# A planned lag before transposes and value products, and a dearer change of tiling, in a fused attention and gated MLP kernel

## The chip, the cores and the metric

The kernel runs on one core of a Trainium2 chip. The metric is the time of one execution on the device in microseconds (us); lower is better. Matrix products run on PE (TensorE), elementwise work on DVE (VectorE), ACT (ScalarE) and a little on POOL (GpSimd); SP issues the loads and stores.

## The reference

Inputs are `q`, `k`, `v` of 4 batches x 8 heads x 768 positions x 64, and three weight matrices of the MLP. In short:

```python
scores = scale * q @ k^T + bias           # bias falls with distance, one slope per head
scores = where(is_global | is_local, scores, -1e9)   # 8 global keys, 96 local keys back
a      = softmax(scores)
x      = (a @ v), heads side by side      # 3072 tokens x 512
out    = ((x @ w_a) * (x @ w_b)) @ w_out  # 512 -> 1536 -> 512
```

Attention is sparse: a block of 128 queries needs the first keys and the 96 before it, so 256 key columns (128 for the first block of a batch). Everything is fp32 on the outside; the large products split each operand in a high and a low part (`xh`, `xl`; `hh`, `hl`; the two halves of `wt`) and add three products. The weights arrive as 64-bit words and are turned into fp32 and split on ACT and DVE first.

## The kernel before

The 24 query blocks of 128 tokens are cut into eight units of 4, 2, 3, 3, 3, 3, 3, 3 blocks. Unit 0's attention stands alone at the start. After it, the MLP of unit *u* runs on PE while the attention of unit *u*+1 is threaded between its matmuls. The MLP of a unit loops over 12 slices `f` of the hidden width: two products `p0`, `p1` (L851, 12 matmuls each), a copy of `p0` by ACT into `raw0` (L341), a product with `p1` on DVE (L890), a split into `hh` and `hl`, and the product back into `acc` (L869).

The attention of one head and one block is a chain over four engines: scores on PE (`ps`, L793; L673 in the first two units), subtraction of the distance and a row minimum on DVE (`t`, L537), the exponential on ACT (L553), a sum and a reciprocal on DVE (`sm`, L568 and L575), the normalisation on ACT, DVE or POOL (`t`, L585 or L587), two transposes on PE into `pt` (L609), a copy into `pf` (L341), and, for all blocks of two heads at once, the product with the values on PE (`pa`, L626). Head *h*+2's operands (`qh`, `ql`, `kk`) are split by DVE and ACT meanwhile. The scores use the array as 128 rows x 128 columns, the values as 128 x 64 (two heads side by side in the array), the scores of the first two units as 64 x 128: each is another tiling of the array.

No order is written by hand. Every step is an `Op` with a due time, a price in ns on each engine that can do it, and the buffers it reads and writes. `Schedule.order` plays the program with these prices: an engine that is free takes, of the steps whose inputs are ready, the one with the earliest due time whose buffers fit; a step's result counts as ready for the next after a lag per engine (`LAGS`: PE 200 ns, ACT 270, DVE 230, POOL 290). What comes out is only the order in which each engine's instructions stand, and which engine does a step that several can do. On the chip each engine then follows its list and waits on semaphores where an input is not there. A step that the plan thinks ready too early therefore holds up everything behind it on its engine, and any change of a price or a lag moves the whole plan from there on.

Transposes are planned by `turn`, value products by `values`; `Plan` holds a unit's blocks, and `paired` is true for units 0 and 1.

Of the kernel before, what the change touches and what calls it, by code (L numbers as in the profile page):

```python
# [24 lines left out]
P = 128  # L25
# [17 lines left out]
SPLITLEAD = 3000  # L43
SLACK = 1.5
BACKLOG = 1.0
PRICE = {"dve": 2.0, "pool": 2.0}
TRACE = False
LAGS = {"pe": 200.0, "act": 270.0, "dve": 230.0, "pool": 290.0, "dma": 2300.0}
# [12 lines left out]
class Plan:  # L61
# [3 lines left out]

    def __init__(self, blocks, paired):
        self.nb = len(blocks)
        self.kkeys = []
        self.vkeys = []
        self.kwin = []  # L70
        self.vslot = []
        self.parts = []
        for n, (b, blk) in enumerate(blocks):
            if blk == 0:
                keys = np.arange(P)
            else:
                q0 = blk * P
                keys = np.concatenate([np.arange(G), np.arange(q0 - LW, q0 + P)])
            joined = blk == 1 and n > 0
            if paired and n % 2 == 0:  # L80
                self.parts.append(len(self.kkeys))
            if joined:
                self.kwin.append((self.kwin[-1][0], 2 * P))
                self.kkeys += [(b, j) for j in keys[P:]]
                self.vslot.append([self.vslot[-1][0], len(self.vkeys)])
                self.vkeys.append((b, keys[P:]))
            else:
                self.kwin.append((len(self.kkeys), len(keys)))
                self.kkeys += [(b, j) for j in keys]
                slots = []  # L90
                for c in range(len(keys) // P):
                    slots.append(len(self.vkeys))
                    self.vkeys.append((b, keys[c * P : (c + 1) * P]))
                self.vslot.append(slots)
        self.nk = len(self.kkeys)
        self.nv = len(self.vkeys)
        self.k0 = self.nb * P
        self.ncol = self.k0 + self.nk // 2
        if paired:

            ends = self.parts[1:] + [self.nk]
            self.pieces = []
            at = 0
            for k, end in zip(self.parts, ends):
                self.pieces.append((at, at + 2 * P - k, 2 * P + end - k, (k, end)))
                at += 2 * P + end - k
            self.ncol = at
# [41 lines left out]


class Op:
    def __init__(self, index, due, costs, emit, reads, writes, late, port):
        self.index, self.due, self.costs, self.emit, self.late = index, due, costs, emit, late
        self.port = port
        self.bufs, self.after, self.before = [], [], 0
        self.ready, self.engine = 0.0, None
        found = {}
        for is_write, keys in ((False, reads), (True, writes)):
            for key in keys:
                buf, part = key if isinstance(key, tuple) else (key, None)  # L160
                if buf not in self.bufs:
                    self.bufs.append(buf)
                for other, p, w in buf.log:
                    if (w or is_write) and other is not self and (p == part or p is None or part is None):
                        found[other.index] = other
                buf.log.append((self, part, is_write))
        for other in found.values():
            other.after.append(self)
            self.before += 1
        for buf in self.bufs:  # L170
            buf.left += 1


class Schedule:
# [11 lines left out]
        self.tags.setdefault(b.tag, []).append(b)  # L186
        return b

    def op(self, due, emit, reads=(), writes=(), late=0.0, port=(), **costs):

        self.ops.append(Op(len(self.ops), due, costs, emit, reads, writes, late, port))

    def order(self):
        free = {e: 0.0 for e in self.SYNC}
        ready = {e: [] for e in self.SYNC}
        heap = []
        head = {t: 0 for t in self.tags}
        live = {t: 0 for t in self.tags}
        taken = set()
        out = []  # L200
        now = 0.0
        port = 0.0

        def arrive(op):
            for e in op.costs:
                insort(ready[e], (op.due, op.index, op))

        def fits(op):
            for b in op.bufs:
                if b in taken:  # L210
                    continue
                queue = self.tags[b.tag]
                if head[b.tag] >= len(queue) or queue[head[b.tag]] is not b or live[b.tag] >= b.bufs:
                    return False
            return True

        def wins(op, e):
            if len(op.costs) == 1:
                return True
            at = {}  # L220
            for o, c in op.costs.items():
                at[o] = max(free[o], now) + c * PRICE.get(o, 1.0)
                for due, index, other in ready[o]:
                    if (due, index) >= (op.due, op.index):
                        break
                    if len(other.costs) == 1 and fits(other):
                        at[o] += BACKLOG * other.costs[o]
            return at[e] <= min(at.values()) + 40.0

        for op in self.ops:  # L230
            if not op.before:
                arrive(op)
        while len(out) < len(self.ops):
            started = True
            while started:
                started = False
                for e in free:
                    if free[e] > now:
                        continue
                    for item in ready[e]:  # L240
                        op = item[2]
                        if e in op.port and port > now:
                            continue
                        if fits(op) and wins(op, e):
                            break
                    else:
                        continue
                    for o in op.costs:
                        ready[o].remove(item)
                    for b in op.bufs:  # L250
                        if b not in taken:
                            taken.add(b)
                            head[b.tag] += 1
                            live[b.tag] += 1
                    op.engine = e
                    op.t0 = now
                    out.append(op)
                    free[e] = now + op.costs[e]
                    if e in op.port:
                        port = free[e]  # L260
                    heappush(heap, (free[e], 0, op.index, op))
                    started = True
            if not heap:
                raise RuntimeError("no order")
            now, kind, _, op = heappop(heap)
            if kind == 0:
                for nxt in op.after:
                    if op.engine == "pe" and tuple(nxt.costs) == ("pe",):
                        lag = 0.0
                    else:  # L270
                        lag = self.SYNC[op.engine] + op.late
                    nxt.ready = max(nxt.ready, now + lag)
                    nxt.before -= 1
                    if not nxt.before:
                        heappush(heap, (nxt.ready, 1, nxt.index, nxt))
                heappush(heap, (now + self.SYNC[op.engine], 2, op.index, op))
            elif kind == 1:
                arrive(op)
            else:
                for b in op.bufs:  # L280
                    b.left -= 1
                    if not b.left:
                        live[b.tag] -= 1
        return out, now
# [21 lines left out]
class Fast:  # L306
# [292 lines left out]
                act=act(w) + 100,  # L599
            )  # L600

    def turn(self, due, wins, t, pt, pf):

        nc = self.nc
        w = sum(w for o, w in wins)

        def emit(e):
            for c in range(0, w, P):
                nc.tensor.transpose(pt[:, c : c + P], t[:, c : c + P], self.ident)  # L609

        self.plan.op(due, emit, [t], [pt], pe=w / P * 109)
        self.copy(due, lambda: pf[:, :w], lambda: pt[:, :w], w, [pt], [pf], psum=True)

    def values(self, due, pl, blocks, v, probs, pa):
# [18 lines left out]

        reads = [v] + [probs[s, i][0] for s in range(2) for i in blocks]
        n = sum(len(pl.vslot[i]) for i in blocks)
        self.plan.op(due, emit, reads, [pa], pe=n * 218 + 200)

    def quad(self, u, c, j, due, raw, v, pa, homes):

# [128 lines left out]
    def attention(self, u, start, end):  # L768
        nc, pl, op = self.nc, PLANS[u], self.plan.op
# [7 lines left out]
        for c in range(NCC):  # L777
            probs = {}
            v = self.fetch_v(u, c, start + (2 * c + 1) * step - LOADLEAD)
            for s in range(2):  # L780
# [4 lines left out]
                for i in range(pl.nb):  # L785
# [18 lines left out]
                    self.softmax(h, due, [(0, w)], ps, t, sm)  # L804
                    pt = self.bank("psT", "pt" + n)
                    pf = self.sbuf([P, 2 * P], F32, "pf", "pf" + n, PFBUFS)
                    self.turn(due, [(0, w)], t, pt, pf)
                    probs[s, i] = (pf, 0)
            due = start + (2 * c + 2) * step
            pa = self.bank("psA", f"pa{u}_{c}")  # L810
# [505 lines left out]
```

## Time and profile before

| | us |
|---|---|
| median of 3 runs (lowest, highest) | 778.75 (777.14, 778.99) |
| the profiled execution's own time | 777.36 |
| its span on the core | 775.1 |
| PE busy | 751.5 (97%) |
| DVE busy | 438.7 (57%) |
| ACT busy | 433.7 (56%) |
| unit 0's attention alone, until the first MLP matmul | 38.1 |
| MLP of the last unit, from 695 us on, nothing threaded in | 74.5 |

PE is the engine that the time goes by, and its busy share is near all of the span; but matmul records overlap, so a late matmul is often hidden in a "busy" PE. Two other readings are needed: the time from the start of one matmul to the start of the next, and the idle time of the weight loads (PEld), which stand in PE's queue and wait there for a late input.

### The profile page before, as it was taken

How to read it: one execution, taken by the hardware profiler on the slowest of the kernel's cores; microseconds unless marked ns; L12 is line 12 of the kernel's file. 1: busy time of each engine (PE TensorE's matmuls, PEld its weight loads, DVE VectorE, ACT ScalarE, POOL GpSimd, SP SyncE). 2: the span in 40 equal slices, each digit the busy share in tenths (PEclk: the TensorE clock that was granted, in tenths of full speed). 3: DMA queues.
4: the chain of work that ended last, by engine and by line, in shares of the span. 5: the costliest groups of instructions: out<-in, count | busy, mean ns of one | idle time of the engine just before them, and what ended most of it. 6: DMA issues, size and time to landing. Idle time of an engine off the chain costs nothing.

```text
span 775.1 us, 12558 instructions
## 1 busy us (share of the span) xinstructions
PE 751.5 (97%) x4608; PEld 663.6 (86%) x4608; DVE 438.7 (57%) x1375; ACT 433.7 (56%) x1093; POOL 6.6 (1%) x24
## 2 busy tenths in 40 slices
PE   5799999999999999999999999999999999999997
PEld 4567777798998998989988988999988999889996
DVE  6999999766655654445554554455554545522111
ACT  6999756466656556455555565555544655442111
POOL 1000000000000000000000000000000000000000
PEclk9999999999999999999999999999999999999999
DMA  7888101032221111211112111111112121000001
GB/s 287 334 321 340 35 14 31 32 107 65 75 90 41 62 38 49 72 48 49 43 54 89 42 62 48 48 60 48 52 42 62 62 62 41 0 28 15 1 1 45
DMA packets 20086, 58.04 MB, mean 75 GB/s; under 512 B 2352, under 2 KB 2608, under 8 KB 20016
## 3 DMA queue, kind: packets, MB, share of 16 engines
q1 hardware_dynamic: 20016, 57.16, 21.5%
q8 instruction: 38, 0.62, 0.3%
q14 instruction: 32, 0.26, 0.1%
HBM read 50.86 MB, written 6.29 MB: 74 GB/s over the span
## 4 chain that ended last, share of the span: by engine, by line
PE 84%; DVE 7%; ACT 6%; issue 1%; DMA 1%; ACTq 0%; DVEq 0%
PE p L851 45%; PE acc L869 23%; PE pt L609 5%; PE pa L626 5%; PE ps L793 4%; PE ps L673 1%; ACT wr L418 1%; DVE kk L351 1%; DVE t L537 1%; ACT t L553 1%; ACT t L585 1%; ACT wm L381 1%; DVE wm L408 1%; ACT pf L341 1%; DVE wt L351 1%
## 5 line engine op out<-in xcount | busy, mean ns | idle before, releaser
L851 PE MATMUL p<-xh,wt 128*128 128x384 f32 (+2 forms) x1488 | 438.9, 345 | 4.0 <-DVE wt L343 2.3
L851 PEld LDWEIGHTS p<-xh,wt 128*128 128x128 f32 x1488 | 272.9, 189 | 18.2 <-issue 3.6
L851 PE MATMUL p<-xl,wt 128*128 128x384 f32 (+2 forms) x816 | 269.8, 342 | 0.2 <-DVE xl L351 0.2
L869 PE MATMUL acc<-wt,hh 128*128 128x512 f32 x576 | 206.4, 397 | 0.0
L851 PEld LDWEIGHTS p<-xl,wt 128*128 128x128 f32 x816 | 153.8, 189 | 10.3 <-DVE xl L351 1.4
L890 DVE TENSOR_TENSOR raw<-p,raw 128x384 f32<-128x384 f32 (+2 forms) x96 | 53.4, 557 | 153.5 <-PE p L851 146.8
L869 PEld LDWEIGHTS acc<-wt,hh 128*128 128x128 f32 x576 | 108.3, 188 | 19.0 <-issue 0.5
L553 ACT ACTIVATE t<-t,sm 128x256 f32<-128x256 f32 (+1 forms) x192 | 93.8, 491 | 40.0 <-DVE sm L537 39.0
L869 PE MATMUL acc<-wt,hl 128*128 128x512 f32 x288 | 113.0, 392 | 0.0
L585 ACT ACTIVATE t<-t,sm 128x256 f32<-128x256 f32 (+1 forms) x140 | 68.7, 494 | 71.1 <-DVE sm L575 66.2
L537 DVE CUSTOM_DVE_ANT_0 t<-ps,rel 128x256 f32<-128x256 f32 x160 | 66.6, 421 | 66.9 <-PE ps L793 64.4
L341 ACT COPY raw<-p 128x384 f32<-128x384 f32 (+2 forms) x95 | 45.3, 477 | 70.7 <-PE p L851 70.1
L609 PE MATMUL pt<-ident,t 128*128 128x128 f32 x352 | 68.6, 280 | 5.3 <-ACT t L585 2.5
L341 ACT COPY pf<-pt 128x256 f32<-128x256 f32 (+3 forms) x151 | 56.2, 375 | 22.6 <-PE pt L609 21.6
L351 DVE TENSOR_TENSOR hl<-raw,hh 128x384 fp32r<-128x384 f32 (+2 forms) x96 | 53.4, 556 | 23.7 <-ACT hh L341 23.1
L609 PEld LDWEIGHTS pt<-ident,t 128*128 128x128 f32 x352 | 43.2, 140 | 25.5 <-ACT t L585 10.1
L341 ACT CAST hh<-raw 128x384 fp32r<-128x384 f32 (+2 forms) x85 | 43.6, 513 | 35.9 <-DVE raw L890 34.9
L869 PEld LDWEIGHTS acc<-wt,hl 128*128 128x128 f32 x288 | 54.2, 188 | 6.6
L568 DVE TENSOR_SCALAR sm<-sm 128x1 f32<-128x1 f32 (+1 forms) x168 | 25.7, 153 | 43.5 <-ACT t L553 42.4
L351 DVE TENSOR_TENSOR kk<-raw,kk 64x384 fp32r<-64x384 f32 (+1 forms) x90 | 44.2, 491 | 2.8
L626 PE MATMUL pa<-pf,v 128*64 128x128 f32 x640 | 42.8, 278 | 2.4 <-ACT pf L341 1.9
L626 PEld LDWEIGHTS pa<-pf,v 128*64 128x64 f32 x640 | 34.7, 136 | 11.6 <-issue 5.0
(78 smaller groups left out, 604.7 us busy)
## 6 DMA issues: line engine op xcount, KB each, us to landing
wr<-wts SPq DMA_DIRECT2D x24, 768.0 KB, 12.5
raw<-qkv SPq DMA_DIRECT2D x29, 384.0 KB, 3.0
raw<-qkv SPq DMA_DIRECT2D x24, 320.0 KB, 2.9
v<-qkv SPq DMA_DIRECT2D x16, 384.0 KB, 3.1
out<-o SPq DMA_DIRECT2D x23, 256.0 KB, 2.1
v<-qkv SPq DMA_DIRECT2D x16, 256.0 KB, 2.7
raw<-qkv SPq DMA_DIRECT2D x3, 640.0 KB, 6.0
raw<-qkv SPq DMA_DIRECT2D x1, 256.0 KB, 3.5
```

Of the source, the lines that this page charges most:

```text
L341: self.nc.scalar.copy(out(), src())
L351: lambda e: self.engine(e).tensor_sub(out(), a(), b()),
L537: lambda e, j=j, o=o, w=w, neg=neg: nc.vector.tensor_tensor_reduce(t[:, o : o + w], ps[:, o : o + w], neg[:, :w], -(2.0 ** -(h + 1)), 3.0e ...
L553: lambda e, j=j, o=o, w=w: nc.scalar.activation(t[:, o : o + w], t[:, o : o + w], AF.Exp, bias=sm[:, j : j + 1], scale=-1.0, accum_out=sm[ ...
L568: lambda e: nc.vector.tensor_scalar_add(sm[:, 2 * n : 3 * n], sm[:, n : 2 * n], 1e-9),
L585: nc.scalar.mul(t[:, o : o + w], t[:, o : o + w], r)
L609: nc.tensor.transpose(pt[:, c : c + P], t[:, c : c + P], self.ident)
L626: nc.tensor.matmul(pa[D * s : D * s + D, i * P : i * P + P], v[:, v0 : v0 + D], pf[:, o + c * P : o + c * P + P], start=c == 0, stop=c == ...
L793: nc.tensor.matmul(ps[:, :w], q[:, i * P : i * P + P], kk[:, k0 : k0 + w], start=m == 0, stop=m == 1,)
L851: nc.tensor.matmul(p[:, :T], wt(), b[:, b0 : b0 + T], start=c == 0 and n == 0, stop=c == NCC - 1 and n == 2,)
L869: nc.tensor.matmul(acc[i][:, :], hs[:, i * P : i * P + P], wt(), start=f == 0 and n == 0, stop=f == NF - 1 and n == 2,)
L890: lambda e, asb=asb, pb=pb: nc.vector.tensor_mul(asb[:, :T], pb[:, :T], asb[:, :T]),
```

## The change

Three edits. First, in units 2 to 7 a transpose and a value product count as ready in the plan only 200 ns (`SPARE`) after their inputs' usual lag has passed. The field that carries this replaces `late`, which was always zero; it is now the lag of the step that waits and not of the step that made the input. Secondly, every value product, in all units, is planned 90 ns dearer on PE (290 ns for the change of tiling, not 200). Thirdly, `Plan` keeps whether its unit is one of the later ones. Nothing is computed differently; only orders and the choice of engines can change.

```diff
+SPARE = 200.0
 ...
     def __init__(self, blocks, paired):
         self.nb = len(blocks)
+        self.late = not paired
 ...
                     if op.engine == "pe" and tuple(nxt.costs) == ("pe",):
                         lag = 0.0
                     else:
-                        lag = self.SYNC[op.engine] + op.late
+                        lag = self.SYNC[op.engine] + nxt.spare
                     nxt.ready = max(nxt.ready, now + lag)
 ...
-    def turn(self, due, wins, t, pt, pf):
+    def turn(self, due, wins, t, pt, pf, spare=0.0):
 ...
-        self.plan.op(due, emit, [t], [pt], pe=w / P * 109)
+        self.plan.op(due, emit, [t], [pt], pe=w / P * 109, spare=spare)
 ...
-        self.plan.op(due, emit, reads, [pa], pe=n * 218 + 200)
+        self.plan.op(due, emit, reads, [pa], pe=n * 218 + 290, spare=SPARE if pl.late else 0.0)
 ...
-                    self.turn(due, [(0, w)], t, pt, pf)
+                    self.turn(due, [(0, w)], t, pt, pf, SPARE)
```

The lines of the changed file stand five lines further down than those of the file before (L609 becomes L614, L851 becomes L856).

The order moves in three places that matter below. The first is PE in the MLP of unit 2, around the transposes of unit 3's head 5, block 2 (`pt3_5_2`); `p02_8` and `p12_8` are the two products of hidden slice 8. Before:

```order
L851 MATMUL p02_8_3274<-xh2_2584,wt8_0_1219 128x384
L851 MATMUL p02_8_3274<-xl2_2593,wt8_0_1219 128x384
L851 MATMUL p02_8_3274<-xh2_2584,wt8_0_1219 128x384
L609 MATMUL pt3_5_2_3325<-ident_91,t3_5_2_3279 128x128 x2
L851 MATMUL p12_8_3282<-xh2_2584,wt8_1_1250 128x384
L851 MATMUL p12_8_3282<-xl2_2593,wt8_1_1250 128x384
L851 MATMUL p12_8_3282<-xh2_2584,wt8_1_1250 128x384
```

Now:

```order
L856 MATMUL p02_8_3283<-xh2_2569,wt8_0_1215 128x384
L856 MATMUL p02_8_3283<-xl2_2586,wt8_0_1215 128x384
L856 MATMUL p02_8_3283<-xh2_2569,wt8_0_1215 128x384
L856 MATMUL p12_8_3291<-xh2_2569,wt8_1_1247 128x384
L856 MATMUL p12_8_3291<-xl2_2586,wt8_1_1247 128x384
L856 MATMUL p12_8_3291<-xh2_2569,wt8_1_1247 128x384
L614 MATMUL pt3_5_2_3330<-ident_91,t3_5_2_3278 128x128 x2
```

Three matmuls of the MLP have moved ahead of the two transposes.

The second place is ACT near the end of unit 0's attention, from the first weight tile's preparation on (`wm`, `wr`: steps of preparing weights; `wt0_0`: the first finished weight tile; `t1_0_3_0`: the normalised probabilities of a head in the fourth pair). Before:

```order
L381 ACTIVATE wm0_0_504<-wr0_0_283 128x768
L418 ACTIVATE wr0_0_283<-wr0_0_283 128x768
L341 CAST xh0_337<-pa0_2_463 128x512
L341 COPY pf0_0_3_0_522<-pt0_0_3_0_509 128x384
L341 COPY pf1_0_3_0_526<-pt1_0_3_0_516 128x384
L381 ACTIVATE wm0_1_528<-wr0_1_317 128x768
L418 ACTIVATE wr0_1_317<-wr0_1_317 128x768
```

Now:

```order
L386 ACTIVATE wm0_0_497<-wr0_0_278 128x768
L346 COPY pf0_0_3_0_510<-pt0_0_3_0_493 128x384
L590 ACTIVATE t1_0_3_0_454<-t1_0_3_0_454,sm1_0_3_0_455 128x128
L590 ACTIVATE t1_0_3_0_454<-t1_0_3_0_454,sm1_0_3_0_455 128x256
L346 CAST xh0_334<-pa0_2_475 128x512
L423 ACTIVATE wr0_0_278<-wr0_0_278 128x768
L346 COPY pf1_0_3_0_525<-pt1_0_3_0_519 128x384
L386 ACTIVATE wm0_1_529<-wr0_1_317 128x768
L423 ACTIVATE wr0_1_317<-wr0_1_317 128x768
L346 CAST wt0_0_543<-wm0_0_497 128x768
```

ACT has gained two normalisations and the cast of the first weight tile; DVE did these before.

The third place is ACT a little later, up to the first copy out of the bank `p0` (`raw0<-p00_0`), which frees that bank for slice 1. Before:

```order
L585 ACTIVATE t1_0_3_1_484<-t1_0_3_1_484,sm1_0_3_1_485 128x256
L418 ACTIVATE wr2_0_433<-wr2_0_433 128x768
L418 ACTIVATE wr2_1_458<-wr2_1_458 128x768
L341 COPY pf0_0_3_1_612<-pt0_0_3_1_594 128x512
L341 COPY pf1_0_3_1_618<-pt1_0_3_1_601 128x512
L381 ACTIVATE wm2_0_620<-wr2_0_433 128x768
L418 ACTIVATE wr3_0_487<-wr3_0_487 128x768
L341 CAST xl0_344<-pa0_3_531 128x512
L341 CAST wt1_0_647<-wm1_0_553 128x768
L418 ACTIVATE wr3_1_514<-wr3_1_514 128x768
L418 ACTIVATE wr4_0_544<-wr4_0_544 128x768
L341 COPY raw0_86<-p00_0_561 128x512
```

Now:

```order
L346 COPY pf0_0_3_1_602<-pt0_0_3_1_593 128x512
L423 ACTIVATE wr1_1_393<-wr1_1_393 128x768
L386 ACTIVATE wm2_0_617<-wr2_0_424 128x768
L346 COPY pf1_0_3_1_619<-pt1_0_3_1_611 128x512
L346 CAST wt1_0_624<-wm1_0_561 128x768
L423 ACTIVATE wr2_0_424<-wr2_0_424 128x768
L423 ACTIVATE wr2_1_457<-wr2_1_457 128x768
L346 CAST xl0_344<-pa0_3_534 128x512
L386 ACTIVATE wm2_1_653<-wr2_1_457 128x768
L346 CAST wt1_1_657<-wm1_1_589 128x768
L423 ACTIVATE wr3_0_488<-wr3_0_488 128x768
L346 COPY raw0_86<-p00_0_553 128x512
```

Ahead of the copy there now stand the cast `wt1_1` and the step `wm2_1`, which came after it, while `wr3_1` and `wr4_0` have moved behind it.

More of the change, by code (lines that the diff above doesn't have):

```diff
@@ L151, with __init__ @@
 class Op:
-    def __init__(self, index, due, costs, emit, reads, writes, late, port):
-        self.index, self.due, self.costs, self.emit, self.late = index, due, costs, emit, late
+    def __init__(self, index, due, costs, emit, reads, writes, spare, port):
+        self.index, self.due, self.costs, self.emit, self.spare = index, due, costs, emit, spare
         self.port = port
@@ L187, in buf, with op @@
         return b
-    def op(self, due, emit, reads=(), writes=(), late=0.0, port=(), **costs):
-        self.ops.append(Op(len(self.ops), due, costs, emit, reads, writes, late, port))
+    def op(self, due, emit, reads=(), writes=(), spare=0.0, port=(), **costs):
+        self.ops.append(Op(len(self.ops), due, costs, emit, reads, writes, spare, port))
     def order(self):
```

## The prediction

> **What bounds the kernel now.** I read the page's head first, then the stretches, then who waits for whom on PE and its weight loads, then the instructions in order of time.
>
> ```profile
> span 775.1 us, 12558 instructions
> PE 751.5 (97%) x4608; PEld 663.6 (86%) x4608; DVE 438.7 (57%) x1375; ACT 433.7 (56%) x1093; POOL 6.6 (1%) x24
> PE 84%; DVE 7%; ACT 6%; issue 1%; DMA 1%; ACTq 0%; DVEq 0%
> ```
>
> PE holds 84% of the chain that ended last. Where the other engines hold it shows in the table of stretches (columns: length, busy time and count of PE, PEld, DVE, ACT, POOL, then granted clock, DMA share, GB/s):
>
> ```profile
> 0.00:38.10 38.10, 25.01 (x208) 17.76 (x208) 29.55 (x145) 30.83 (x95) 2.20 (x18) 0.96 0.80 309
> 38.10:50.70 12.60, 10.89 (x57) 7.71 (x57) 12.14 (x24) 12.45 (x20) 0.00 (x0) 0.86 0.75 278
> 50.70:156.00 105.30, 104.70 (x516) 82.43 (x517) 99.90 (x194) 75.14 (x136) 0.00 (x0) 1.00 0.29 112
> 227.00:322.00 95.00, 94.46 (x592) 85.63 (x592) 49.48 (x167) 53.22 (x140) 0.74 (x1) 1.00 0.17 51
> ```
>
> Until 50.7 us PE is not the bound: in the second stretch DVE (12.1 of 12.6 us) and ACT (12.45) are full and PE issues 57 rows. From 50.7 on PE is, with DVE at 95% in the rest of unit 0's MLP and about half busy later. So two kinds of gain or loss count: whatever moves the 50.7, and every late input of PE behind it.
>
> The late inputs of the units from the third on show as waits of weight loads, which stand in PE's queue (engine, what, released by: us, times, longest; from 160 to 770 us):
>
> ```profile
> PEld pt L609 <- ACT t L585: 8.8, 23, 0.8
> PEld pa L626 <- issue: 4.0, 13, 0.4
> PEld p L851 <- DVE xl L351: 1.4, 5, 0.5
> PEld pt L609 <- ACT pf L341: 1.6, 5, 0.3
> ```
>
> Transposes (`pt`) wait for the normalisation; value products (`pa`) wait for no input of theirs. One late transpose, in order of time:
>
> ```profile
> 287.45 0.74 DVE L343 CAST kk<-raw 64x384 fp32r<-64x384 f32 x2
> 287.76 0.34 PE L851 MATMUL p<-xh,wt 128*128 128x384 f32 x1
> 287.94 0.38 PE L609 MATMUL pt<-ident,t 128*128 128x128 f32 x2
> 288.08 0.42 PE L851 MATMUL p<-xh,wt 128*128 128x384 f32 x1
> 290.05 0.17 DVE L575 RECIPROCAL sm<-sm 128x1 f32<-128x1 f32 x1
> 290.32 0.34 PE L851 MATMUL p<-xh,wt 128*128 128x384 f32 x1
> 290.60 0.51 ACT L585 ACTIVATE t<-t,sm 128x256 f32<-128x256 f32 x1 [1.87 <-DVE sm L537]
> 291.16 0.44 PE L609 MATMUL pt<-ident,t 128*128 128x128 f32 x2 [0.50 <-ACT t L585]
> 291.35 0.42 PE L851 MATMUL p<-xh,wt 128*128 128x384 f32 x1
> ```
>
> A matmul of 384 columns is followed by the next start after 0.18 us (287.76 to 287.94). At 290.32 it is followed after 0.84: 0.66 us are lost, because DVE split the next head's keys before it did the reciprocal (290.05) and ACT normalised only then. The pair of transposes itself then takes 0.19 to the next start and not 0.14. "Idle" says 0.50 here and PEld's wait 0.82, so I use starts.
>
> **Part one: the lag before transposes.** How much is there to gain? 23 waits of 8.8 us, each some 0.16 longer than what PE loses (0.82 against 0.66): 8.8 - 23 x 0.16 = 5.1, and 23 x 0.05 for the slower pair: 6.3 us. Counted block by block from the spacing of starts, 26 of the 144 transposes of units 2 to 7 start 0.04 us or more late, in all 5.6 us; with 26 x 0.05 that is 6.9. I take 6.9 as the pool.
>
> The new order tells how much of it goes. I laid each block's transposes beside its scores and summed the PE rows between them at the spacings above (0.174 us for 384 columns, and in proportion). The mean distance grows from 3.58 to 3.73 us, less than the 0.20 asked for, since PE can only move them by whole steps of three matmuls (0.52 us). Of the 26 late ones 12 stand 0.39 to 0.71 us further off, as `pt3_5_2` does by three matmuls; they hold 3.4 of the 5.6 us, and with 12 x 0.05 that is **-4.0**. 14 stand as before, with 2.3 us; in three of them (block 2 of head 2, units 3, 5 and 7) one cast of keys has left DVE's list between the minimum and the reciprocal, 0.37 us each (two in 0.74 above), more than their 0.20 us of lateness: another **-0.7**. 20 blocks that are on time come closer, for instance `pt5_0_0` and `pt7_0_0` from 5.73 to 3.08 us and `pt2_4_0` from 3.10 to 2.65. The shortest distances that start on time now are 2.8, so a handful become late by 0.1 to 0.3: **+0.6**. Sum of part one: -4.1. Its bounds: -1.5, if as many new ones come late as in the moved list are cured (12 x 0.2 against 4.0); -6.9, if all of the pool goes.
>
> What the moved transposes delay is the copy `pf` and the value products, which have nobody waiting on PE (above); the scores of the next block need another bank and do not stand behind them.
>
> **Part two: the lag and the dearer price of value products.** One visit to the other tiling:
>
> ```profile
> 292.42 0.40 PE L869 MATMUL acc<-wt,hh 128*128 128x512 f32 x1
> 292.75 1.53 PE L626 MATMUL pa<-pf,v 128*64 128x128 f32 x24
> 294.21 0.44 PE L609 MATMUL pt<-ident,t 128*128 128x128 f32 x2
> 295.02 0.39 PE L869 MATMUL acc<-wt,hh 128*128 128x512 f32 x1
> 295.25 0.39 PE L869 MATMUL acc<-wt,hl 128*128 128x512 f32 x1
> ```
>
> Entering costs 0.33 - 0.23 = 0.10 us over the usual spacing of 512 columns, the 24 rows and the way out 1.46: 1.56 in all. The plan charged 6 x 0.218 + 0.20 = 1.51, now 1.60; one is as wrong as the other. The number of value products and of changes of tiling on PE is the same in both orders (87), so no visit is saved. Since they never waited, the lag has nothing to take away. I cost this at 0 in units 2 to 7. What hides it: the result `x` is needed only at the next unit's start, some 10 us after the last block. If that cover went, one value product late by the lag would cost 0.2 + 0.09 us in each of six units: +1.7 at most.
>
> **Part three: what the dearer price does to unit 0.** The 290 holds there too, and from the fourth pair of heads on the orders differ. Here ACT sets PE's start:
>
> ```profile
> 24.01 0.41 ACT L585 ACTIVATE t<-t,sm 128x128 f32<-128x128 f32 x1
> 24.31 0.51 ACT L553 ACTIVATE t<-t,sm 128x256 f32<-128x256 f32 x1
> 35.53 0.98 ACT L418 ACTIVATE wr<-wr 128x768 int32<-128x768 uint32 x1
> 36.33 0.56 ACT L553 ACTIVATE t<-t,sm 128x256 f32<-128x256 f32 x1
> 41.50 0.88 ACT L341 CAST wt<-wm 128x768 fp32r<-128x768 f32 x1
> 42.22 0.57 ACT L585 ACTIVATE t<-t,sm 128x256 f32<-128x256 f32 x1
> 42.63 1.79 ACT L418 ACTIVATE wr<-wr 128x768 int32<-128x768 uint32 x2
> 50.08 0.56 ACT L341 COPY raw<-p 128x512 f32<-128x512 f32 x1
> 50.69 0.50 PE L851 MATMUL p<-xh,wt 128*128 128x512 f32 x1 [0.66 <-ACT raw L341]
> ```
>
> By the starts, a weight step costs ACT 0.80 us, a cast of a weight tile 0.72, a normalisation 0.41 (256 columns) or 0.30 (128). Between the first `wm0_0` and the copy `raw0` ACT gains `wt0_0`, `wt1_1`, `wm2_1`, one normalisation of 128 and two of 256, and loses `wr3_1` and `wr4_0`: 0.72 + 0.72 + 0.80 + 0.30 + 0.82 - 1.60 = +1.76. Before `wm0_0` it loses two normalisations of 256 (to DVE): -0.82. If ACT stays as full as it is, the copy, and with it slice 1 on PE, comes 0.94 later: **+1.0**. Bounds: +1.8, if the 0.82 turns into a wait for DVE, which has taken those two; -0.5, if DVE, freed of the cast `wt0_0` and the two halves of `t1_0_3_0`, lets waits vanish that I do not see.
>
> Sum: -4.1 + 0 + 1.0 = -3.1 us. The profiled execution took 777.36 (span 775.1, and 2.3 around it), so 774.3 for it; it lay 1.4 below the median of the runs, and the same step from the median gives **775.7 us**, 0.4% less. About 0.3%, 2.3 us, is what a measurement of this kernel can tell from no change.
>
> **The rivals.** *The gain is given back in place.* Each plan that moves 87 blocks makes new late ones: 20 come closer, and DVE does five more normalisations of 256 columns over the whole kernel. If part one ends at its lower bound, -1.5 + 1.0: **778.2**, no change. For it speaks that more than half of the late ones stand where they stood; against it that the large ones (0.66, 0.47, four of 0.36 to 0.38) moved.
>
> *The weights become the bound.* In unit 0's MLP DVE is busy 99.9 of 105.3 us; four subtractions of keys and a few casts have moved onto it from POOL and ACT, some 2.5 us at 0.3 to 0.55 each (the cast above is 0.37). It decides once a weight tile's lead over its first matmul is used up: from there each us on DVE is one on PE. Price: the head at +1.8, and the stage by what DVE needs above 105.3 with the waits that it has now, 2.5 to 5 more; with part one as forecast 777.36 - 4.1 + 1.8 + 5 = 780.1, from the median **781.5**, slower. Against it: PE stands with no idle to speak of in that stretch (104.7), so the lead exists.
>
> *A wait in the head drops the clock.*
>
> ```profile
> 35.80:39.20 3.40, 0.73 (x3) 1.00 1.03 422
> 39.20:42.60 3.40, 2.73 (x6) 0.56 1.01 415
> ```
>
> (Columns: PE alone, clock, DMA share, GB/s.) After a stretch in which PE had three rows, the clock stands at 0.56 for the next 3.4 us: 1.5 us lost, though now beside ACT's work. If the longer wait for `raw0` does the same again, it falls on the dense matmuls behind it, where nothing hides it: +1.5, **777.2**. The Trainium skill, "TensorE: Matmul & The Clock Gate", Part 1, says that an idle window of some 3.4 us halves the array's clock until a busy one has passed; this trace agrees with 0.56.
>
> **How the numbers follow.** Forecast 0.52, 775.7 (own range 773.6 to 777.2); given back 0.27, 778.2; clock 0.08, 777.2; weights as the bound 0.13, 781.5. The forecast ends faster by over 0.3% (below 776.4) in some 0.43 of its 0.52, the given-back and clock cases in 0.05 together: faster 0.48, slower 0.12 (nearly all of the weights case), same 0.40. The range goes from 772.8 (part one near its upper bound with the head at 0.5) to 779.8, where half of the slower case is left out.
>
> **What would show it.** Right: PEld's waits for the normalisation between 160 and 770 us fall from 8.8 to some 4 us, `pt3_5_2` starts 0.18 after its forerunner, and slice 1 on PE starts near 51.7 and not 50.7. Wrong: a wait sum that stays near 8, or new waits at `pt` behind DVE's own normalisations; slice 1 before 50.7; or PE idle behind `wt` between 51 and 156 us.

## The result, and the profile after

The changed kernel takes 772.97 us in the median of six runs (771.42 to 774.44), the kernel before 778.82 (777.14 to 778.99). The ratio is 0.993 with a 95% interval of 0.9916 to 0.9943: 5.85 us less, about twice the 3.1 forecast. The time lies 0.2 us inside the range (772.8 to 779.8) and below the narrower one that the prediction gave its forecast (773.6 to 777.2). The two profiled executions lie 4.2 us apart (777.36 and 773.14), nearer to the forecast than the medians are; part of what parts them is told below.

The head of the page of the changed kernel, and its row for the transposes:

```profile
span 771.4 us, 12534 instructions
PE 750.4 (97%) x4608; PEld 666.3 (86%) x4608; DVE 441.0 (57%) x1383; ACT 431.2 (56%) x1088; POOL 4.0 (1%) x21
PE 94%; ACT 3%; DVE 2%; DMA 0%; issue 0%; DVEq 0%; ACTq 0%
L614 PE MATMUL pt<-ident,t 128*128 128x128 f32 x352 | 67.1, 277 | 2.9 <-DVE sm L573 2.0
```

The span is 3.7 us shorter with PE's busy share unchanged: the late matmuls were counted as busy, so this share could not show them. The chain that ended last is PE's own to 94% now, from 84%; this share hangs on the path that the chain takes through the start as well, and the kernel with a lag of 800 ns below has 88%.

Who waits in the queue of PE's weight loads between 160 and 770 us (engine, what, released by: us, times, longest):

```profile
PEld pa L631 <- issue: 5.2, 17, 0.4
PEld pt L614 <- ACT t L590: 3.1, 10, 0.5
PEld p L856 <- DVE xl L356: 1.0, 3, 0.5
PEld pt L614 <- ACT pf L346: 0.8, 3, 0.3
```

The transposes' wait for the normalisation fell from 8.8 us in 23 to 3.1 in 10. The block that the prediction took apart, `pt3_5_2`, in PE's order of time:

```profile
289.92 0.34 PE L856 MATMUL p<-xl,wt 128*128 128x384 f32 x1
290.10 0.34 PE L856 MATMUL p<-xh,wt 128*128 128x384 f32 x1
290.27 0.41 PE L614 MATMUL pt<-ident,t 128*128 128x128 f32 x2
290.44 0.42 PE L856 MATMUL p<-xh,wt 128*128 128x384 f32 x1
```

It starts 0.17 us after its forerunner; before, that was 0.84.

The head of the program, ACT and PE, where slice 1 of unit 0's MLP starts:

```profile
51.85 0.59 ACT L346 COPY raw<-p 128x512 f32<-128x512 f32 x1
52.49 0.50 PE L856 MATMUL p<-xh,wt 128*128 128x512 f32 x1 [0.63 <-ACT raw L346]
```

It starts at 52.5 us, 1.8 later than in the first profile, released by the same copy on ACT.

For all further comparisons I use one sum, taken in the same way from each trace: over the 144 blocks of units 2 to 7, how much later than usual the first transpose starts after the row ahead of it (blocks late by 0.04 us or more), plus what the second transpose of a pair then takes over its 0.109 us. Before, 26 blocks are late by 5.63 us and second transposes cost 1.91: 7.54. After, 10 blocks by 1.53, and 0.93: 2.46.

### The profile page after: what moved, and what is told of

Read it like the earlier page. It is cut to its first block, busy times and chain, and to the rows that moved or that the text cites. A ratio compares the mean times of both kernels' runs of the same rounds, so it can differ in the third digit from the quotient of the medians.

```text
span 771.4 us, 12534 instructions
## 1 busy us (share of the span) xinstructions
PE 750.4 (97%) x4608; PEld 666.3 (86%) x4608; DVE 441.0 (57%) x1383; ACT 431.2 (56%) x1088; POOL 4.0 (1%) x21
## 4 chain that ended last, share of the span: by engine, by line
PE 94%; ACT 3%; DVE 2%; DMA 0%; issue 0%; DVEq 0%; ACTq 0%
PE p L856 52%; PE acc L874 25%; PE pa L631 5%; PE pt L614 5%; PE ps L798 4%; PE ps L678 2%; ACT wr L423 1%; DVE t L542 0%; DMA nv<-ns 0%; DVE kk L356 0%; ACT wm L386 0%; ACT pf L346 0%; ACT t L590 0%; ACT t L558 0%; ACT wt L346 0%
## 5 line engine op out<-in xcount | busy, mean ns | idle before, releaser
L856 PE MATMUL p<-xh,wt 128*128 128x384 f32 (+2 forms) x1488 | 439.7, 346 | 2.0 <-ACT wt L346 1.4
L856 PEld LDWEIGHTS p<-xh,wt 128*128 128x128 f32 x1488 | 273.2, 189 | 16.5 <-issue 3.9
L856 PE MATMUL p<-xl,wt 128*128 128x384 f32 (+2 forms) x816 | 270.4, 342 | 1.1 <-ACT xl L346 0.7
L856 PEld LDWEIGHTS p<-xl,wt 128*128 128x128 f32 x816 | 154.3, 189 | 10.9 <-ACT xl L346 1.1
L895 DVE TENSOR_TENSOR raw<-p,raw 128x384 f32<-128x384 f32 (+2 forms) x96 | 53.4, 556 | 120.5 <-PE p L856 115.7
L558 ACT ACTIVATE t<-t,sm 128x256 f32<-128x256 f32 (+1 forms) x192 | 93.7, 490 | 41.5 <-DVE sm L542 40.5
L590 ACT ACTIVATE t<-t,sm 128x256 f32<-128x256 f32 (+1 forms) x135 | 66.0, 492 | 63.3 <-DVE sm L580 60.4
L614 PE MATMUL pt<-ident,t 128*128 128x128 f32 x352 | 67.1, 277 | 2.9 <-DVE sm L573 2.0
L356 DVE TENSOR_TENSOR hl<-raw,hh 128x384 fp32r<-128x384 f32 (+2 forms) x96 | 53.4, 557 | 24.2 <-ACT hh L346 23.4
L614 PEld LDWEIGHTS pt<-ident,t 128*128 128x128 f32 x352 | 44.3, 140 | 19.2 <-issue 5.2
L356 DVE TENSOR_TENSOR kk<-raw,kk 64x384 fp32r<-64x384 f32 (+1 forms) x94 | 45.8, 487 | 2.9
L631 PEld LDWEIGHTS pa<-pf,v 128*64 128x64 f32 x640 | 34.7, 137 | 12.7 <-issue 6.0
## 6 DMA issues: line engine op xcount, KB each, us to landing
wr<-wts SPq DMA_DIRECT2D x24, 768.0 KB, 12.5
```

What stands on the lines that cost most here:

```text
L356: lambda e: self.engine(e).tensor_sub(out(), a(), b()),
L558: lambda e, j=j, o=o, w=w: nc.scalar.activation(t[:, o : o + w], t[:, o : o + w], AF.Exp, bias=sm[:, j : j + 1], scale=-1.0, accum_out=sm[ ...
L590: nc.scalar.mul(t[:, o : o + w], t[:, o : o + w], r)
L631: nc.tensor.matmul(pa[D * s : D * s + D, i * P : i * P + P], v[:, v0 : v0 + D], pf[:, o + c * P : o + c * P + P], start=c == 0, stop=c == ...
L856: nc.tensor.matmul(p[:, :T], wt(), b[:, b0 : b0 + T], start=c == 0 and n == 0, stop=c == NCC - 1 and n == 2,)
L895: lambda e, asb=asb, pb=pb: nc.vector.tensor_mul(asb[:, :T], pb[:, :T], asb[:, :T]),
```

## The experiments

Every kernel was timed beside the kernel before on the same chip; that kernel's own median went from 778.3 to 779.4 us, so ratios compare better than times. The edits are against the changed kernel, unless said. All start with one of two heads, that is, orders of the start of the program. In the kernels that keep the price of 200 in units 0 and 1, PE's rows in the trace have the forms of the kernel before up to row 843 of 4608 (some 165 us); in the one other, the price alone, they have those of the change up to row 850.

### One part at a time

**The lag of the transposes alone.**

```diff
-        self.plan.op(due, emit, reads, [pa], pe=n * 218 + 290, spare=SPARE if pl.late else 0.0)
+        self.plan.op(due, emit, reads, [pa], pe=n * 218 + 200, spare=0.0)
```

> Only the lag of 200 ns before transposes in units 2 to 7; value products as in the kernel before (200 ns, no lag). The first 707 matmul rows of PE stand as in the kernel before, so unit 0 and its MLP cost what they did. Theory (late transposes are the gain): of the 26 late ones 12 move by over 0.3 us, as in the change; lateness falls from 5.6 to some 1.5 us, slice 1 starts at 50.7 us, and the time is 778.8 - 4.9 = 773.9 (772.5 to 775.3). Rival (the dearer price brings the gain because the plan then fits the chip): 778.8, no change. Rival (any reshuffle moves the time by a few us whatever it does to the transposes): the time has no tie to the lateness in the trace.

Measured: 772.63 us, ratio 0.9919 (0.9905 to 0.9932), 8 blocks late by 0.83 us. Its wait row for the normalisation is

```profile
PEld pt L614 <- ACT t L590: 2.3, 8, 0.4
```

The whole gain, and perhaps a little more, comes with this part alone; the first theory holds and the price as the cause does not.

**The dearer price alone.**

```diff
-        self.plan.op(due, emit, reads, [pa], pe=n * 218 + 290, spare=SPARE if pl.late else 0.0)
+        self.plan.op(due, emit, reads, [pa], pe=n * 218 + 290, spare=0.0)
 ...
-                    self.turn(due, [(0, w)], t, pt, pf, SPARE)
+                    self.turn(due, [(0, w)], t, pt, pf)
```

> Only the price of 290 ns for a value product, in all units; no lag anywhere. The first 714 matmul rows of PE stand as in the change. Theory: the head is the change's (slice 1 near 52.5 us, 1.8 later than before), the late transposes stay (5 to 6 us of lateness), so the time is 778.8 + 0.7 to + 1.8 = 779.5 to 780.6. Rival (the price brings the gain): 773 to 775.

Measured: 777.28 us, ratio 0.998 (0.9971 to 0.9989): a small gain where I expected a small loss. Its wait row for the normalisation is

```profile
PEld pt L614 <- ACT t L590: 7.8, 21, 0.6
```

and its sum of lateness 6.35, so 1.2 us of the 1.5 go with transposes that the new plan moved, though it gives them no lag. The head starts slice 1 at 53.4 us and yet nothing of it is left in the time. That contradicts part three of the prediction; I return to it below.

**The lag of the value products alone.**

```diff
-        self.plan.op(due, emit, reads, [pa], pe=n * 218 + 290, spare=SPARE if pl.late else 0.0)
+        self.plan.op(due, emit, reads, [pa], pe=n * 218 + 200, spare=SPARE if pl.late else 0.0)
 ...
-                    self.turn(due, [(0, w)], t, pt, pf, SPARE)
+                    self.turn(due, [(0, w)], t, pt, pf)
```

> Only the lag of 200 ns before value products in units 2 to 7, price 200. Theory: value products never waited for an input, the late transposes stay as they are: 778.8, within 1.5. If the lag of the value products had a part in the gain: 777 or less.

Measured: 778.38 us, ratio 0.9999 (0.999 to 1.0008). Nothing, as expected: 26 blocks are late, as before.

**The change without its price in units 0 and 1.**

```diff
-        self.plan.op(due, emit, reads, [pa], pe=n * 218 + 290, spare=SPARE if pl.late else 0.0)
+        self.plan.op(due, emit, reads, [pa], pe=n * 218 + (290 if pl.late else 200), spare=SPARE if pl.late else 0.0)
```

> The change, with the dearer price held back from units 0 and 1 (200 there, 290 from unit 2 on). The first 707 rows of PE stand as in the kernel before. Theory: the head's loss goes (slice 1 at 50.7 and not 52.5), the gain of the transposes stays: 0.7 to 1.8 below the change's 773.0, so 771.2 to 772.3. If what the head loses is made up later anyway: 773.0.

Measured: 773.35 us, ratio 0.993 (0.9917 to 0.9944), the change's own. Slice 1 starts at 50.7 us, 1.8 earlier than in the change, and the end is no earlier. The second case holds: what the head loses is made up.

### Is it lateness, or any other plan?

**The kernel before, once more.** No edit.

> The kernel before, word for word, profiled once more: a control for two things that a single profile can't tell. Slice 1 of unit 0's MLP started at 50.7 us in the first profile and at 50.7, 51.6 and 52.2 in the three variants whose rows stand the same up to there; if the head scatters by itself, it lies anywhere in 50.5 to 52.5. The 384-column matmuls of the last unit stood 173.4 ns apart in the first profile and 176.7 in the change: if that belongs to the chip or the moment and not to the change, 176 to 177 shows here too. Time 778.7, the same.

Measured: 778.74 us, ratio 1.0001 (0.9992 to 1.0011), 7.47 us of lateness. Slice 1 starts at 51.9 us. Two things scatter between executions of the same program; they stand under the unexpected.

**The lag for the third block of each head alone, and for the other two alone** (both with price and value products as before).

```diff
-                    self.turn(due, [(0, w)], t, pt, pf, SPARE)
+                    self.turn(due, [(0, w)], t, pt, pf, SPARE if i == pl.nb - 1 else 0.0)
```

> Lag of 200 ns for the transposes of the third block of each head alone (units 2 to 7); price and value products as before. 24 of the 26 late transposes belong to third blocks; 11 late ones move by over 0.3 us. Theory (lateness is the gain): lateness 5.6 to some 1.5, time 778.7 - 4.5 = 774.2 (773.0 to 775.5). Rival (any lag or reshuffle helps in proportion to what it moves): a third of the transposes moved, a third of the gain, 776.7.

```diff
-                    self.turn(due, [(0, w)], t, pt, pf, SPARE)
+                    self.turn(due, [(0, w)], t, pt, pf, SPARE if i < pl.nb - 1 else 0.0)
```

> The complement: lag of 200 ns for the transposes of the first and second block alone. Theory: these were on time, what moves with them cures some third blocks by chance (6 of the late ones stand over 0.3 us further off), lateness 3.5 to 5, time 776 to 778. Rival (in proportion to what is moved): two thirds of the gain, 774.7.

Measured: 775.70 us, ratio 0.9962 (0.9948 to 0.9975), and 775.41, ratio 0.9959 (0.9945 to 0.9973). Both miss what I said: the first takes 1.5 us more than the 774.2, 0.2 above its range, and the second is 0.6 below its own, 776 to 778. The rival does worse. It had 776.7 and 774.7, the second 2.0 faster; the means of five runs each are 0.3 apart, with some 0.9 either way. Their wait rows for the normalisation are

```profile
PEld pt L614 <- ACT t L590: 5.0, 14, 0.6
```

```profile
PEld pt L614 <- ACT t L590: 6.3, 18, 0.7
```

My expectation for the first failed on the lateness itself: 15 blocks stay late, by 2.95 us and not 1.5. With second transposes the lateness left is 4.09 us in the first and 5.01 in the second, which the times do not tell apart; so lateness explains a time to about 1 us and no finer. What is shown is that the number of blocks that carry the lag does not set the gain. That moving any block also moves the splits and copies of the others, and so cures some and delays some, is my reading.

**The lag with its sign turned.** The transposes' lag alone, and

```diff
-SPARE = 200.0
+SPARE = -200.0
```

> The lag of transposes in units 2 to 7 with its sign turned: 200 ns earlier than in the kernel before; value products as before. The transposes stand 0.23 us nearer their scores in the mean, the 26 late ones 0.39 us. Theory (lateness sets the time): the late ones lose 26 x 0.39 = 10 us more and many that were just on time become late: 788 to 803 us. Rival (any reshuffle of the plan moves the time by a few us, of either sign): 775 to 781.

Measured: 783.14 us, ratio 1.0054 (1.0036 to 1.0073). It is slower by 4 us and not by 10 or more, between the two ranges. The time alone does not part theory and rival, since a few us of either sign were allowed to the rival; the trace does. It has 34 blocks late by 9.99 us and 2.24 on second transposes, 4.7 more than before. Its wait rows:

```profile
PEld pt L614 <- ACT t L590: 12.5, 27, 0.8
PEld pt L614 <- ACT hh L346: 3.2, 4, 0.8
```

I had sized it by rows between scores and transposes, and that failed. The 26 blocks that were late before do stand 0.4 us nearer to their scores in the trace, but their normalisation ends some 0.4 us sooner as well, and their lateness goes from 5.6 us to about 4.8. The increase is in some 14 other blocks, about 5.2 us in all. Distance in PE's order alone does not give lateness.

### How much lag

All with the transposes' lag alone (price and value products as before), but for the last.

```diff
-SPARE = 200.0
+SPARE = 400.0
```

> Lag of 400 ns before all transposes of units 2 to 7, price and value products as before. Theory: 16 late ones move by over 0.3 us, lateness under 0.6, time 772.0 (771.2 to 772.8): hardly less than with 200, since little is left. If the longer lag is paid for in later value products or in buffers held longer: 773 or more.

> Lag of 600 ns before transposes alone. Theory: with 400 ns some 0.4 us of lateness and 0.7 of slow second transposes are left, so at most 1 us more is to be had: 770.5 to 771.5. If a longer lag is paid for elsewhere: over 772.

> Lag of 800 ns before transposes alone: the mean distance grows from 3.58 to 4.26 us. Theory: no lateness is left to take, 770.5 to 771.5, and any price of the lag shows here first: waits for the banks of the scores or of the transposes, or value products that wait for their copies; then 772 to 775.

Measured: 771.33 us, ratio 0.9903 (0.989 to 0.9917); 770.69, ratio 0.9891 (0.9874 to 0.9907); 770.32, ratio 0.9891 (0.9874 to 0.9907). The first two lie within what was expected, the third 0.2 us below it. At 800 ns no row `pt` behind ACT's normalisation is left among the waits; the five largest rows are

```profile
PEld pa L631 <- issue: 5.2, 18, 0.4
PEld p L856 <- issue: 1.9, 11, 0.2
PEld pt L614 <- issue: 1.9, 11, 0.2
PEld pa L631 <- DMA raw<-qkv: 0.8, 3, 0.3
PEld p L856 <- DVE xl L356: 0.5, 1, 0.5
```

No new wait of more than 0.2 us has come in, and the one that grew, before the value products (4.0 us in 13 before), stood at 5.2 in the change too; so a price of the longer lag did not show up to 800 ns. From 600 on there is little left to take: 0.76 and 0.67 us of lateness.

The change's pair with 400 ns, price held back from units 0 and 1:

```diff
-SPARE = 200.0
+SPARE = 400.0
 ...
-        self.plan.op(due, emit, reads, [pa], pe=n * 218 + 290, spare=SPARE if pl.late else 0.0)
+        self.plan.op(due, emit, reads, [pa], pe=n * 218 + (290 if pl.late else 200), spare=SPARE if pl.late else 0.0)
```

> Lag of 400 ns before transposes and value products and the price of 290 in units 2 to 7, unit 0 and 1 as before. With 200 ns the same pair stood at 773.35 (with price and value lag) and 772.63 (without), so what they add is nothing or a small loss: 771.3 to 772.5, beside 771.3 without.

Measured: 771.81 us, ratio 0.9908 (0.9891 to 0.9925); with 400 ns, too, the price and the value products' lag add nothing.

### All of them beside their lateness

| kernel | late blocks | lateness, us | less than before | ratio (95%) |
|---|---|---|---|---|
| lag -200 | 34 | 12.23 | -4.7 | 1.0054 (1.0036 to 1.0073) |
| before | 26 | 7.54 | | |
| value lag alone | 26 | 7.17 | 0.4 | 0.9999 (0.999 to 1.0008) |
| price alone | 24 | 6.35 | 1.2 | 0.998 (0.9971 to 0.9989) |
| lag, first two blocks | 19 | 5.01 | 2.5 | 0.9959 (0.9945 to 0.9973) |
| lag, third block | 15 | 4.09 | 3.5 | 0.9962 (0.9948 to 0.9975) |
| price late units, lags | 9 | 2.57 | 5.0 | 0.993 (0.9917 to 0.9944) |
| the change | 10 | 2.46 | 5.1 | 0.993 (0.9916 to 0.9943) |
| lag 200 | 8 | 1.79 | 5.8 | 0.9919 (0.9905 to 0.9932) |
| lag 400 | 4 | 1.13 | 6.4 | 0.9903 (0.989 to 0.9917) |
| lag 400, price late units, value lag | 4 | 1.05 | 6.5 | 0.9908 (0.9891 to 0.9925) |
| lag 600 | 2 | 0.76 | 6.8 | 0.9891 (0.9874 to 0.9907) |
| lag 800 | 1 | 0.67 | 6.9 | 0.9891 (0.9874 to 0.9907) |

1% is 7.8 us. The time follows the lateness through the whole table, within 1 us up to a lag of 200; at 400, 600 and 800 it falls by 7.6, 8.5 and 8.5 us and the lateness by 6.4, 6.8 and 6.9. Most of that difference stands in the traces too. A row of the MLP right behind transposes or value products takes some 0.09 us longer than usual to the next start (in the prediction's lines 291.35 to 291.61, 0.26 for 0.174). From 160 us on this makes 13.7 us in the kernel before, 13.8 in the change, and 12.6, 12.7 and 12.5 with the lag at 400, 600 and 800, where fewer MLP rows stand right behind a transpose (132, 127 and 131, not 140). That is some 1.1 us more; what is left, up to 0.7, stays open. With the lag at -200 the same sum is 13.0, which brings its 4.7 to 4.0, beside 4.2 by the ratio. The ratio of the change's own median, 0.993, is 5.5 to 5.9 us for 5.1 of lateness.

The kernels with a lag of 600 or 800 ns before transposes and nothing else of the change, both at a ratio of 0.9891, are the fastest and beat both kernels; which of the two is better the runs do not tell.

## Why the prediction was right, and where it was not

**The bound and the pool: right.** PE with a late input ahead of it was what there was to gain. The pool was put at 6.9 us; the same trace gives 7.5 with all second transposes counted.

**Part one, the lag before transposes: right in mechanism, too small by 1.0.** -4.1 was forecast; the traces give 7.54 - 2.46 = 5.1. Of the twelve late blocks that the order moved away, eleven are on time. The twelfth, `2_7_2`, moved by 0.7 us and is still 0.29 late, because its normalisation ends 0.7 later too. On time, too, are the three from which a cast of keys left DVE's list. Of the eleven others, which moved little or not at all, I had left all as they were: four are cured (320 ns of `2_5_2`, 385 of `6_5_2`, 68 and 95 of `3_0_2` and `4_5_2`), because the normalisation came earlier: by the traces it ends 0.70, 0.40, 0.15 and 0.13 us sooner after the block's scores. One grew (`5_1_2`, 135 to 390 ns), with its normalisation 0.28 later. New late ones came to 0.3 us (`2_1_2`, `2_4_2`) and not 0.6; the blocks named as in danger, `5_0_0`, `7_0_0` and `2_4_0`, start on time. (The lower bound of part one, 12 x 0.2 against 4.0, is -1.6 and not -1.5; nothing hangs on it.) Reading only PE's side of the order, but for those three blocks, was the step that fell short: lateness is the chain's end minus PE's arrival, and both ends move.

**Part two, value products: right.** The lag alone gives 0.9999. The price in the later units gives no gain: 773.35 with price and value lag, 772.63 without.

**Part three, the head: the delay was right, its cost was not.** Slice 1 does start later, by the ACT rows that were counted: 52.5 and 53.4 us in the two profiles with that head, 50.3 to 52.2 (mean 51.4) in twelve with the old one, so +1.5 where +1.0 was forecast. But it is not paid at the end. From the start of slice 1 to that of slice 11 the old head needs 94.6 to 95.3 us, the new one 93.9 in both. What went is two late pairs of unit 1's own transposes, in PE's order of time in the kernel before:

```profile
71.75 0.38 PE L609 MATMUL pt<-ident,t 128*128 128x128 f32 x2
72.35 0.44 PE L609 MATMUL pt<-ident,t 128*128 128x128 f32 x2 [0.22 <-ACT t L585]
94.37 0.38 PE L609 MATMUL pt<-ident,t 128*128 128x128 f32 x2
95.14 0.44 PE L609 MATMUL pt<-ident,t 128*128 128x128 f32 x2 [0.39 <-ACT t L585]
```

and after, where all four or eight transposes run in one piece:

```profile
72.83 0.60 PE L614 MATMUL pt<-ident,t 128*128 128x128 f32 x4
95.71 1.03 PE L614 MATMUL pt<-ident,t 128*128 128x128 f32 x8
```

Two pairs of transposes are 0.22 us apart when on time; these were 0.60 and 0.77 apart. 0.4 + 0.55 = 0.9 us, nearly all of the 1.1, and it is the order that does it: the old head keeps its 95 us when slice 1 starts at 52.2, too. I had not looked at unit 1's transposes, as the change gives them no lag; the dearer price moved them all the same. Net, the head costs 0.5 us or so in the traces; the time of the price alone shows none of it.

**The sum.** -4.1 + 1.0 = -3.1 against -5.85 measured. So the cause and the way were right and the size was about half of what came: 1.0 us more came from the transposes, and the head cost 0.5 to 1.0 less. Both errors point the same way, which is why the time came near the end of the range. The other 0.8 to 1.3 us of the difference are not assigned; single profiles scatter by as much (last section). For the profiled pair alone the gain is 4.2.

**The rivals.** That the gain is given back in place did not happen: 0.3 us of new lateness. The weights did not become the bound: after 53 us one weight load of PE waits behind `wt`, for 0.3 us. The clock rival fell as well; in stretches of 3.4 us of the changed kernel's head (length, PE busy, clock, DMA share, GB/s)

```profile
34.40:37.80 3.40, 1.52 (x14) 0.77 0.88 314
37.80:41.20 3.40, 3.40 (x9) 0.50 1.02 411
41.20:44.60 3.40, 3.40 (x14) 0.73 0.95 387
48.00:51.40 3.40, 2.48 (x13) 1.00 0.70 231
51.40:54.80 3.40, 2.77 (x12) 1.00 1.00 403
```

the clock is down where it was before, beside ACT's work, and at full rate behind the wait for `raw0`. It is at half rate from 36.2 to 43.1 us, 6.8 us; the kernel before had 3.4 us of this in its first profile and 6.8 in its second. The Trainium skill, "TensorE: Matmul & The Clock Gate", Part 1, has the halved clock follow an idle window of some 3.4 us. The 0.69 and 0.63 us that PE waits ahead of 52.5 us are well short of that, and no drop follows them in the trace. The drop at 36.2 us does not fit such a window if it has to be idle throughout. The longest times that PE stood idle around it are 1.28 and 1.40 us:

```profile
34.89 0.88 PE L631 MATMUL pa<-pf,v 128*64 128x128 f32 x12 [1.28 <-DVE xl L735]
37.16 0.80 PE L856 MATMUL p<-xh,wt 128*128 128x512 f32 x1 [1.40 <-ACT wt L346]
```

How much idle time brings a drop, these runs do not show.

## What to carry to other kernels

Where a planner fixes each engine's order, a step that it believes ready too early stalls all that stands behind it on a full in-order engine, while one planned a little late costs nothing as long as other work is at hand: give the bound engine's waiting steps a safety lag, and raise it until the waits are gone, as long as no new one comes (here they were nearly gone at 400 to 600 ns, and none came up to 800). Look for such waits in the spacing of starts and in the weight loads' queue, not in the busy share. And before a delay at the start is counted against the end, follow it to the next place where the same engine waits.

## What the runs showed that was not expected

The start of the MLP scatters by itself: in twelve executions whose rows stand the same up to there, slice 1 begins between 50.3 and 52.2 us. The spell in which the clock falls to half rate is part of it. In the seven of the twelve that have a whole 6.8 us of it behind the first MLP matmul, slice 1 comes 13.7 to 14.0 us after that matmul; in the other five, with 3.4 to 5.5 us of it, 12.5 to 12.8. Why the spell differs stays open. The kernel before in its first and its second profile (length, PE busy, clock, DMA share, GB/s):

```profile
38.10:50.70 12.60, 10.89 (x57) 0.86 0.75 278
```

```profile
38.10:50.70 12.60, 11.11 (x55) 0.74 0.76 287
```

The last unit, where nothing but the MLP runs, has three speeds at a granted clock of 1.00. The 24 matmuls of 384 columns of one slice, from the chain in order of time, in the first profile of the kernel before, in its second, and in the changed kernel:

```profile
723.88 4.16 PE p L851 x24
```

```profile
718.99 4.19 PE p L851 x24
```

```profile
719.39 4.24 PE p L856 x24
```

That is 173.4, 174.7 and 176.7 ns from start to start, and 62.3, 62.7 and 63.1 us from slice 1 to slice 11. The kernel before shows two of the three, so the change does not decide it; I do not know what does. It puts 0.8 us between the two profiles that the prediction and its result rest on.

A late pair of transposes costs more than its wait: the second then takes 0.16 to 0.17 us and not 0.11, which makes 1.9 us in all in the kernel before.
